# Evictions ahead of the phases, or behind them: one reordered loop in a fused state-space and MLP kernel

## The chip, the cores and the metric

The kernel runs on one core of a Trainium2 chip. The metric is the device time of one execution in microseconds (us), and the median of several executions is what is compared. The core's engines run side by side, each through its own list of instructions in a fixed order, and they meet only at semaphores: TensorE (PE in the profile, its weight loads PEld), VectorE (DVE), ScalarE (ACT), GpSimd (POOL) and SyncE (SP), which here only issues transfers.

## What is computed

The reference is a block with two branches, with one row of conditioning `c` that scales and shifts both (2048 positions, 512 channels, 128 states). Cut to what matters:

```python
mod = silu(c) @ w_mod                       # six rows of 512: sa, ca, ga, sb, cb, gb
h = layernorm(u) * (1 + ca) + sa
K = real(sum_n C * dt*B * exp(dt*A * l))    # a kernel of 2048 taps for each channel
x = u + ga * (causal_conv(h, K) + h * Dskip)
h = layernorm(x) * (1 + cb) + sb
x1 = h + shift(gelu(layernorm(h) @ w1)) @ w2
x = x + gb * (x1 + gelu(layernorm(x1) @ w3) @ w4)
```

`dt` is `exp(log_dt)`; `A`, `B` and `C` are complex. The reference does the convolution with FFTs of length 4096; the kernel does it with matrix multiplications by small DFT matrices.

## The kernel before, in words

All of it is fp32, with products split in two parts where accuracy asks for it. It goes in this order: a preparation (to about 46 us); the **generation stage** (about 46 to 258 us), which makes the 512 x 2048 taps of K and, beside it, normalises u and takes the first DFT of u; the spectra and their products; the inverse transforms; the two halves of the MLP.

The change is in the generation stage. Its loop (L530) runs `k` from 0 to 32; steps 0 to 31 each make the taps of one group of 16 channels of a quarter, and every fourth step is `fresh` (k = 1, 5, 9, ...), which makes the exponentials for the next four steps. The tasks of one step are these:

- `turns(k, cos)` (L452): eight or ten matmuls into a PSUM tile `xx` of 128 x 1024 (the phases, in turns), which ACT turns into `sn` or `cs` with one Sin (L464, recorded at L118, the helper that all ACT work shares). There are two `xx` tiles. The step works two steps ahead: step k issues the phases of step k + 2.
- `exps` (L240): matmuls into the same `xx` tiles, and an Exp by ACT into `p`. The change from Sin to Exp and back costs a table load on ACT.
- `products(k)` (L469): seven DVE operations that multiply `sn`, `cs` and `p` into `e0` and `e1` (two buffers each).
- `burst(k)` (L493): 64 small matmuls of `e1` by `e0` into `kp`. At odd k the tile is full, and an eviction by ACT (`kp` to `KX`) is put off into the list `later`.
- `u_dft` (L431): eight matmuls of the normalised u into two PSUM tiles `pu`, and an eviction put off into `later`: two ACT copies to `vs`, and four transfers of them to DRAM by SP. There are two `pu` tiles, so one `u_dft` fills both. It runs at the end of 16 of the steps.
- `mod_parts` and `mod_sum` (L213, L222): for three of the six rows of the conditioning, matmuls into `pu` and an ACT copy put off into `later` (to `wm` and `modg`).
- `fill` (L488): matmuls whose result is overwritten.

The lists of the engines are written out by hand: the stage stands under `manual_schedule`, so each engine executes its instructions in the order in which the Python code issues them. The matmuls are issued when a task is called; what a task puts into `later` is issued in the next step, as `now`. PE's order in a step is therefore: phases of k + 2, in a fresh step two of the `exps`, `burst(k)`, in a fresh step the rest of the `exps` with `fill`, then `u_dft` or the rows of the conditioning. ACT's order in a step before the change is: `sn` and `cs` of k + 2, the evictions of the step before, and in a fresh step the Exps.

Of the kernel before, what the change touches and what calls it, by code (L numbers as in the profile page):

```python
# [109 lines left out]
def body(ctx, tc, A):  # L110
# [129 lines left out]
    def exps(t, u0, u1):  # L240
        if u0 == 0:
            PE[t] = [], pe.tile([128, 4, 16, NX1], F32, name="p1")
        p0, p1 = PE[t]
        for u in range(u0, u1):
            x = psx.tile([128, 1024], F32, name="xx")
            if u == 4:
                for i, n in ((0, 512), (512, 64 * NX1)):
                    T.matmul(x[:, i:n], TES[:, t], CE[:, 1024 + i:1024 + n], start=True, stop=True)
                act(p1.rearrange("p u d c -> p (u d c)"), x[:, :64 * NX1], AF.Exp)
                continue  # L250
            l = TES[u * 32:u * 32 + 32, t]
            for i in range(2):
                T.matmul(x[:, i * 512:i * 512 + 512], l, CE[u * 32:u * 32 + 32, i * 512:i * 512 + 512],  # L253
                         start=True, stop=True)
            p0.append(pe.tile([128, 2, 512], F32, name="p0", bufs=6))
            act(p0[u].rearrange("p a b -> p (a b)"), x, AF.Exp)

    def weigh(t):
        q1 = PE[t][1][:, :, :, 8:12].rearrange("p a b c -> p (a b) c")
        V.tensor_mul(q1, q1, WN[:, t * 64:(t + 1) * 64, None].to_broadcast([128, 64, 4]))  # L260
# [191 lines left out]
    def turns(k, cos):  # L452
        t, u = divmod(k, 4)
        r0 = slice(u // 2 * 64, u // 2 * 64 + 64)
        r1 = slice(64 - r0.start, 128 - r0.start)
        l0, l1, c = T0S[r0, t], T1S[r1, t * 2 + k % 2], slice(k % 2 * 512, k % 2 * 512 + 512)
        x = psx.tile([128, 1024], F32, name="xx")
        ops = [(l0, C0[r0, c], l1, C1[r1])] + [(ON[r0, i], MG[r0], ON[r1, i], MG[r1]) for i in (2, 0, 1)[1 - cos:]]
        ops.append((l0, C0N[r0, c], l1, C1N[r1]))
        for i, (la, ma, lb, mb) in enumerate(ops):  # L460
            T.matmul(x[:, :512], la, ma, start=(i == 0), stop=(i == len(ops) - 1))  # L461
            T.matmul(x[:, 512:], lb, mb, start=(i == 0), stop=(i == len(ops) - 1))  # L462
        o = wk.tile([128, 2, 512], F32, name="cs" if cos else "sn", bufs=3)
        act(o.rearrange("p a b -> p (a b)"), x, AF.Sin, scale=-TWO_PI, bias=hpi if cos else 0.0)  # L464
        return o
# [3 lines left out]
    def products(k):  # L469
        t, u = divmod(k, 4)  # L470
        sn, cs = trig.pop(k)
        mg, pt = PE[t][0][u], PE[t][1][:, u]
        e0 = wk.tile([128, 2, 2, 512], F32, name="e0")
        e1 = wk.tile([128, 2, 16, 32], F32, name="e1")
        f2 = lambda z: z.rearrange("p a b -> p (a b)")
        m1 = wk1.tile([128, 16, 32], F32, name="m1")
        V.tensor_mul(m1.rearrange("p d (x y) -> p d x y", x=4),
                     pt[:, :, None, :8].to_broadcast([128, 16, 4, 8]),
                     pt[:, :, 8:12, None].to_broadcast([128, 16, 4, 8]))
        for a in range(2):  # L480
            V.scalar_tensor_tensor(e0[:, 1, a], sn[:, 0], 1.0 - 2.0 * a, mg[:, a], op0=OP.mult, op1=OP.mult)  # L481
        V.tensor_mul(f2(e1[:, 1]), sn[:, 1], f2(m1))
        V.tensor_mul(e0[:, 0], cs[:, 0:1].to_broadcast([128, 2, 512]), mg)
        V.tensor_mul(f2(e1[:, 0]), cs[:, 1], f2(m1))
        return e0, e1


    def fill(n):  # L488
        for _ in range(n):
            T.matmul(KP[1].rearrange("p a b -> p (a b)"), TES[:, 0], CE[:, :512], start=True, stop=True,  # L490
                     skip_group_check=True)

    def burst(k, e0, e1):  # L493
        if k % 2 == 0:
            KP[0] = KP.pop(1) if 1 in KP else psk.tile([128, 8, 64], F32, name="kp")
        kp = KP[0]
        for g in range(4):
            for r in range(2):
                for j in range(4):
                    d = j * 4 + g  # L500
                    T.matmul(kp[32 * j:32 * j + 32, (k % 2) * 4 + g], e1[:, r, d],  # L501
                             e0[:, r, :, d * 32:d * 32 + 32],
                             start=(r == 0), stop=(r == 1), skip_group_check=True)
        if k % 2 == 1:
            g0 = (k // 2) * 8
            later.append(lambda: act(Kq[:, g0 // 64, g0 % 64:g0 % 64 + 8], kp))
# [19 lines left out]
    with tc.manual_schedule():  # L526
        for k in range(2):
            trig[k] = turns(k, 0), turns(k, 1)
        weigh(0)
        for k in range(33):  # L530
            now, later = later, []
            if 1 in KP:
                fill(3)
            if k + 2 < 32:
                trig[k + 2] = turns(k + 2, 0), turns(k + 2, 1)
            for f in now:
                f()
            if k < 32:
                fresh = k % 4 == 1 and k < 28
                if fresh:  # L540
                    exps(k // 4 + 1, 0, 2)
                e = products(k)
                burst(k, *e)
                if fresh:
                    KP[1] = psk.tile([128, 8, 64], F32, name="kp")
                    fill(3)
                    for u in range(2, 5):
                        exps(k // 4 + 1, u, u + 1)
                        fill(2)
                if k % 4 == 3 and k < 28:  # L550
                    weigh(k // 4 + 1)
            for f in side[k]:
                f()
        for f in later:
            f()
        V.tensor_add(Kq[:, :, :, 31], DS.rearrange("p (h g) -> p h g", h=2), Kq[:, :, :, 31])
        T2 = [up.tile([128, 16, 128], F32, name="xu") for i in range(2)]
        load_t2 = lambda i: Y.dma_start(T2[i], A["T2"].rearrange("p (a b) -> p a b", a=32)[:, i * 16:i * 16 + 16])
        load_t2(0)
# [482 lines left out]
```

## Time and profile before

| | us |
|---|---|
| median of 3 executions | 814.51 |
| lowest, highest | 814.46, 819.1 |
| span of the profiled execution | 817.4 |
| PE busy | 725.9 (89%) |
| DVE busy | 511.1 (63%) |
| ACT busy | 339.0 (41%) |

The time of the profiled execution itself is not listed apart; its span is the nearest to it, and it lies between the median and the highest. The span counts from the first to the last instruction. Busy times are of instructions as the profiler recorded them; the ends of matmuls are modelled, so that the busy share of PE is not its share of peak. "PEclk" is the share of the full TensorE clock that was granted. A row of the timeline has the start, the duration, the engine, the line, the operation with its tiles (written from read), and in brackets how long the engine was idle before it and what ended that wait.

### The profile page before, as it was taken

The numbers are of one execution on the slowest core, as the hardware profiler recorded it, in microseconds if no ns is written. First come the engines' busy times: TensorE is split into PE (matmuls) and PEld (weight loads), VectorE is DVE, ScalarE is ACT, GpSimd is POOL, SyncE is SP. The second block draws the span as 40 slices with busy tenths as digits, with TensorE's granted clock in tenths as the row PEclk, the third lists the DMA queues.
The fourth block names the chain that finished last, engine by engine and source line by source line (L and its number), as shares of the span: only waits on it lengthen the run. The fifth ranks groups of instructions, "written<-read, shape, count | busy, mean of one in ns | idle before, by whom it ended". The sixth has DMA issues, their size and how long they took to land. (4 is left out here: it accounts for less than half of the span.)

```text
span 817.4 us, 17349 instructions
## 1 busy us (share of the span) xinstructions
PE 725.9 (89%) x7340; PEld 550.9 (67%) x7340; DVE 511.1 (63%) x883; ACT 339.0 (41%) x540; POOL 92.5 (11%) x186
## 2 busy tenths in 40 slices
PE   3798999889888989999459899999999999999994
PEld 1355555545556956565248788888888888888883
DVE  8999888768765355777479988543526271714211
ACT  3677676656755344453134554221322122222220
POOL 1011111011000000010026331010101010101000
PEclk9999999989998599999769899999999999999997
DMA  8421152421415999495803453010101010101011
GB/s 294 147 53 41 26 145 53 116 68 28 117 40 131 246 250 311 146 307 182 287 1 121 160 177 118 26 53 1 52 1 53 1 52 1 26 1 26 1 26 26
DMA packets 51046, 79.88 MB, mean 98 GB/s; under 512 B 5172, under 2 KB 37816, under 8 KB 49432
## 3 DMA queue, kind: packets, MB, share of 16 engines
q1 hardware_dynamic: 44808, 57.92, 25.6%
q0 software_dynamic: 6160, 20.85, 8.1%
q8 instruction: 58, 0.95, 0.5%
q14 instruction: 20, 0.16, 0.1%
HBM read 52.53 MB, written 26.21 MB: 96 GB/s over the span
## 5 line engine op out<-in xcount | busy, mean ns | idle before, releaser
L871 DVE TENSOR_TENSOR gl<-gf,gh 128x512 fp32r<-128x512 f32 (+1 forms) x48 | 30.4, 644 | 150.5 <-ACT gh L118 150.5
L118 ACT ACTIVATE gf<-pm 128x512 f32<-128x512 f32 (+1 forms) x48 | 27.0, 562 | 182.1 <-PE pm L865 178.4
L865 PE MATMUL pm<-nh,w3l 128*128 128x256 f32 (+1 forms) x352 | 98.5, 280 | 0.0
L864 PE MATMUL pm<-nl,w3h 128*128 128x256 f32 (+1 forms) x352 | 98.5, 280 | 0.0
L863 PE MATMUL pm<-nh,w3h 128*128 128x256 f32 (+1 forms) x352 | 98.4, 279 | 0.0
L876 PE MATMUL pa<-w4h,gh 128*128 128x512 f32 (+1 forms) x176 | 73.8, 419 | 3.2 <-ACT gh L118 0.9
L877 PE MATMUL pa<-w4l,gh 128*128 128x512 f32 (+1 forms) x176 | 69.6, 396 | 0.0
L863 PEld LDWEIGHTS pm<-nh,w3h 128*128 128x128 f32 (+1 forms) x352 | 65.4, 186 | 1.8
L865 PEld LDWEIGHTS pm<-nh,w3l 128*128 128x128 f32 (+1 forms) x352 | 65.4, 186 | 1.1
L864 PEld LDWEIGHTS pm<-nl,w3h 128*128 128x128 f32 (+1 forms) x352 | 65.2, 185 | 0.6
L878 PE MATMUL pa<-w4h,gl 128*128 128x512 f32 (+1 forms) x176 | 64.2, 396 | 0.0
L481 DVE SCALAR_TENSOR_TENSOR e<-sn,p 128x512 f32<-128x512 f32 x64 | 41.3, 686 | 33.5 <-ACT sn L118 14.2
L461 PE MATMUL xx<-MG,ON 64*128 64x512 f32 x160 | 51.0, 416 | 0.0
L462 PE MATMUL xx<-MG,ON 64*128 64x512 f32 x160 | 50.9, 415 | 0.0
L118 ACT ACTIVATE sn<-xx 128x1024 f32<-128x1024 f32 x32 | 32.9, 1027 | 40.9 <-issue 34.4
L884 POOL DMA_DIRECT2D out<-KX x32 | 16.1, 508 | 257.6 <-DVE KX L882 257.5
L876 PEld LDWEIGHTS pa<-w4h,gh 128*128 128x128 f32 (+1 forms) x176 | 33.0, 188 | 17.9 <-ACT gh L118 13.2
L770 PE MATMUL pm<-nl,w1h 128*128 128x256 f32 x128 | 39.0, 305 | 6.6 <-DVE nl L741 6.6
L643 DVE TENSOR_TENSOR ma<-pk,us 128x512 f32<-128x512 f32 x32 | 21.9, 685 | 29.3 <-issue 21.3
L118 ACT ACTIVATE p<-xx 128x1024 f32<-128x1024 f32 (+1 forms) x40 | 37.8, 981 | 5.1 <-PE xx L253 3.3
L501 PEld LDWEIGHTS kp<-e,e 128*32 128x32 f32 x2048 | 30.5, 111 | 13.1 <-issue 8.5
L769 PE MATMUL pm<-nh,w1h 128*128 128x256 f32 x128 | 39.3, 307 | 0.0
(222 smaller groups left out, 1910.7 us busy)
## 6 DMA issues: line engine op xcount, KB each, us to landing
VU<-vs SPq DMA_DIRECT2D x64, 128.0 KB, 2.4
ld<-VU SPq DMA_DIRECT2D x32, 256.0 KB, 8.7
ZT<-z POOLq DMA_DIRECT2D x16, 512.0 KB, 4.4
ld<-ZT SPq DMA_DIRECT2D x16, 512.0 KB, 5.4
wst<-in_w SPq DMA_DIRECT2D x18, 256.0 KB, 3.3
xu<-in_u SPq DMA_DIRECT2D x16, 256.0 KB, 6.6
KX<-in_u SPq DMA_DIRECT2D x16, 256.0 KB, 9.7
GD<-go POOLq DMA_DIRECT2D x16, 256.0 KB, 3.3
```

The source lines that it names most:

```text
L118: return S.activation(out, in_, f, bias=bias, scale=scale)
L461: T.matmul(x[:, :512], la, ma, start=(i == 0), stop=(i == len(ops) - 1))
L462: T.matmul(x[:, 512:], lb, mb, start=(i == 0), stop=(i == len(ops) - 1))
L481: V.scalar_tensor_tensor(e0[:, 1, a], sn[:, 0], 1.0 - 2.0 * a, mg[:, a], op0=OP.mult, op1=OP.mult)
L769: T.matmul(p[:, e], W1h[:, k, c], hi[k], start=(k == 0), stop=False)
L770: T.matmul(p[:, e], W1h[:, k, c], lo[k], start=False, stop=False)
L863: T.matmul(p[:m, e], W3h[:, k, c], hi[k], start=(k == 0), stop=False)
L864: T.matmul(p[:m, e], W3h[:, k, c], lo[k], start=False, stop=False)
L865: T.matmul(p[:m, e], W3l[:, k, c], hi[k], start=False, stop=(k == 3))
L876: T.matmul(acc[i], gh[:m, e, s], W4h[:m, f], start=(f == 0), stop=False)
L877: T.matmul(acc[i], gh[:m, e, s], W4l[:m, f], start=False, stop=False)
L878: T.matmul(acc[i], gl[:m, e, s], W4h[:m, f], start=False, stop=(f == 10))
```

## The change

In each step the put-off evictions (`now`) are issued ahead of the phases of k + 2, where they were issued behind them.

```diff
             now, later = later, []
             if 1 in KP:
                 fill(3)
+            for f in now:
+                f()
             if k + 2 < 32:
                 trig[k + 2] = turns(k + 2, 0), turns(k + 2, 1)
-            for f in now:
-                f()
             if k < 32:
                 fresh = k % 4 == 1 and k < 28
```

What `now` issues are ACT copies and SP's transfers, and the phases issue matmuls and ACT's Sins. So the order changes on ACT alone; the lists of PE, DVE, POOL and SP hold the same instructions in the same order as before. ACT's order in a step becomes: evictions of the step before, `sn` and `cs` of k + 2, and in a fresh step the Exps. Where a table load for Sin follows the Exps, the eviction of `kp` (and of `pu`, in some of these steps) comes ahead of that load.

## The prediction

> **What bounds the kernel now.** I first read the busy times by stretches, to see how large the stage of the change is and which engine fills it.
>
> ```profile
> 46.00:258.00 212.00, 188.09 (x2905) 115.50 (x2901) 169.27 (x259) 141.79 (x165) 20.12 (x32) 0.94 0.28 68
> ```
>
> The columns are the stretch, its length, busy PE, PEld, DVE, ACT and POOL, the granted TensorE clock, DMA share and GB/s. The stage takes 212.0 us. PE is busy for 188.1 of them, DVE for 169.3, ACT for 141.8: PE is the fullest, but has 24 us of gaps. What ends them is in the view of waits, PE's in this stage:
>
> ```profile
> PE pu L438 <- ACT vs L118: 9.0, 7, 2.3
> PE pu L217 <- ACT vs L118: 3.9, 3, 2.3
> PE xx L253 <- ACT cs L118: 3.3, 7, 0.5
> PE xx L253 <- ACT p L118: 2.3, 5, 0.7
> PE pu L224 <- ACT wm L118: 1.9, 2, 1.2
> PE pu L438 <- ACT modg L118: 1.5, 2, 1.3
> ```
>
> (Total us, times, longest.) The first two and the last two are one cause: PE wants a `pu` tile that ACT has not evicted yet. They make 9.0 + 3.9 + 1.9 + 1.5 = 16.3 us in 14 waits, two thirds of PE's gaps. The timeline of ACT for steps 7 to 9 shows why the eviction is late.
>
> ```profile
> 93.41 1.11 ACT L118 ACTIVATE cs<-xx,hpi 128x1024 f32<-128x1024 f32 x1 [0.16 <-ACT sn L118]
> 96.60 1.03 ACT L118 ACTIVATE sn<-xx 128x1024 f32<-128x1024 f32 x1 [2.08 <-PE xx L462]
> 97.75 1.11 ACT L118 ACTIVATE cs<-xx,hpi 128x1024 f32<-128x1024 f32 x1
> 98.77 0.59 ACT L118 ACTIVATE KX<-kp 128x512 f32<-128x512 f32 x1
> 99.24 1.09 ACT L118 ACTIVATE vs<-pu 128x512 f32<-128x512 f32 x2
> 102.68 1.03 ACT L118 ACTIVATE sn<-xx 128x1024 f32<-128x1024 f32 x1 [2.35 <-issue]
> 103.82 1.11 ACT L118 ACTIVATE cs<-xx,hpi 128x1024 f32<-128x1024 f32 x1
> 104.84 1.08 ACT L118 ACTIVATE vs<-pu 128x512 f32<-128x512 f32 x2
> 105.93 1.28 ACT L118 ACT_TABLE_LOAD   x1
> ```
>
> PE in the same time:
>
> ```profile
> 93.25 1.10 PE L501 MATMUL kp<-e,e 128*32 128x64 f32 x64
> 94.28 1.09 PE L438 MATMUL pu<-xu,FU 32*64 32x512 f32 x8
> ...
> 96.11 0.39 PE L461 MATMUL xx<-C0N,T0S 64*128 64x512 f32 x1
> ...
> 97.59 1.10 PE L501 MATMUL kp<-e,e 128*32 128x64 f32 x64
> 99.89 1.57 PE L438 MATMUL pu<-xu,FU 32*64 32x512 f32 x8 [1.20 <-ACT vs L118]
> 101.39 0.50 PE L461 MATMUL xx<-C,T0S 64*128 64x512 f32 x1
> ...
> 102.20 0.39 PE L461 MATMUL xx<-C0N,T0S 64*128 64x512 f32 x1
> ```
>
> The burst of step 7 ends at 94.35 and its `pu` tiles are full at 95.37. ACT is idle from 94.52 to 96.60, but stands at `sn`, whose phases end at 96.50. It copies `kp` and `pu` only after `sn` and `cs`, from 98.77 to 100.33. PE, through with the next burst at 98.69, waits 1.20 us for the tiles. Then ACT idles again, 2.35 us, put down to "issue": `sn` at 102.68 follows the last phase matmul of 102.20 + 0.39. So each waits for the other in turn. The 14 waits of `sn` of this kind:
>
> ```profile
> ACT sn L118 <- issue: 34.4, 14, 4.1
> ```
>
> **The change part by part.** Only ACT's order changes: no instruction is added or taken away, and the transfers of `vs` go out in the same order on SP, only earlier. POOL's queue isn't passed.
>
> *The evictions in the new place.* In step 8, `kp` is copied at 94.52 to 95.11, as its burst is done, and the two `vs` copies (1.09) run from about 95.4 to 96.5. `sn` could start at 96.60 as before. The work of 1.56 us fits into the 2.08 us of idle ACT, with 0.1 us to spare. It is the same at the other places, since on PE the phases always stand right behind the `u_dft`: they take 1.2 us (95.30 to 96.50 here), the copies 1.09. Should the hand-over between engines take 0.1 us more than this, 16 pairs cost 16 x 0.1 = 1.6 us; I charge that. Its ends are 0 and 16 x 1.09 = 17.4 (all copies on the path).
>
> *PE's waits for `pu`.* With the tiles free by 96.5, `u_dft` of step 8 starts at 98.6 without a wait. All 16.3 us go. A waiting `u_dft` also runs longer, since its second half waits for the second copy: 1.57 against 1.09 us above. There are six of 1.57, the first and the last being these:
>
> ```profile
> 73.14 1.57 PE L438 MATMUL pu<-xu,FU 32*64 32x512 f32 x8 [1.20 <-ACT vs L118]
> ...
> 253.41 1.57 PE L438 MATMUL pu<-xu,FU 32*64 32x512 f32 x8 [0.71 <-ACT vs L118]
> ```
>
> That is 6 x 0.48 = 2.9 us.
>
> *The Exps.* In step 9 the table load stands behind `vs` (104.84 to 105.92). Now it follows `cs` at once, up to 1.1 us earlier, and the waits of `exps` for `p` (2.3 us in the rows above) go too; the 3.3 for `cs` stay. After the Exps, `kp` is copied while ACT waits for phases, so the Sin load isn't later.
>
> The sum so far is 16.3 + 2.9 + 2.3 = **21.5 us**.
>
> *What is late next.* DVE. Its waits in the stage:
>
> ```profile
> DVE e L481 <- ACT sn L118: 14.2, 6, 3.9
> DVE e L481 <- PE kp L501: 13.6, 7, 3.7
> DVE e L481 <- ACT cs L118: 5.7, 2, 4.2
> DVE p L260 <- ACT p L118: 4.9, 4, 1.9
> ```
>
> They add to 38.4 us, and each is a wait for ACT or PE, which come earlier. A saving of 21 to 30 us leaves DVE 8 to 17 us of slack; above 38 there is nothing. I charge nothing for it and keep half of the 21.5 as the other end, for lack of slack early on: until 79 us DVE has hardly any.
>
> ```profile
> 46.00:79.00 33.00, 30.36 (x481) 19.05 (x481) 32.45 (x52) 24.27 (x27) 5.00 (x8) 1.00 0.18 44
> ```
>
> *The clock.* The granted clock falls to about half in six stretches:
>
> ```profile
> 82.00:87.00 5.00, 5.00 (x15) 3.15 (x13) 4.96 (x10) 3.19 (x4) 1.43 (x2) 0.66 0.25 55
> 110.00:114.00 4.00, 4.00 (x13) 2.51 (x11) 2.00 (x5) 1.93 (x3) 0.00 (x0) 0.57 0.74 194
> 147.00:152.00 5.00, 5.00 (x72) 3.25 (x70) 3.94 (x7) 1.65 (x2) 1.09 (x2) 0.66 0.01 3
> 175.00:182.00 7.00, 6.92 (x42) 3.67 (x46) 4.49 (x7) 1.77 (x4) 1.09 (x2) 0.53 0.36 77
> 208.00:214.00 6.00, 6.00 (x92) 3.88 (x92) 1.84 (x3) 2.15 (x3) 0.00 (x0) 0.72 0.65 146
> 236.00:241.00 5.00, 4.93 (x34) 2.92 (x38) 2.40 (x3) 1.53 (x3) 0.00 (x0) 0.66 0.51 107
> 260.00:287.00 27.00, 27.00 (x492) 25.92 (x486) 10.30 (x16) 8.98 (x18) 0.00 (x0) 0.51 1.05 256
> ```
>
> The lost time is length x (1 - clock). The last four in the stage each follow a long wait for `pu`, as at 175:
>
> ```profile
> 175.08 2.46 PE L438 MATMUL pu<-xu,FU 32*64 32x512 f32 x8 [2.27 <-ACT vs L118]
> ```
>
> They lose 5 x 0.34 + 7 x 0.47 + 6 x 0.28 + 5 x 0.34 = 8.4 us, the first two 3.4. If the waits bring the stretches on, the 8.4 go with them; that they do is read from what follows what, and isn't shown. I take half, 4.2; the ends are 0 and 8.4 + 3.4 = 11.8. The stretch from 260 belongs to the next stage, whose start looks the same after the change; I leave it.
>
> [...]
>
> Sum: 21.5 + 4.2 - 1.6 = **24 us**. The profiled execution's span, 817.4, is 2.9 above the median of 814.51; taking the saving off its own span gives 793.3, off the median 790.5. I forecast the median: **790.5 us**.
>
> **The rivals.**
> - *The half-clock stretches stay.* For it: the two at 82 and 110 follow no wait for `pu`. Against: the other four do. The clock term is 0: 814.5 - 21.5 + 1.6 = 794.6 us. [...]
> - *All of the lost clock comes back.* 814.5 - 21.5 - 11.8 + 1.6 = 782.8 us. It needs PE to have no larger gaps left, and DVE to follow at 8 us of slack.
> - *DVE takes over.* PE's waits for `pu` come back as waits of the burst for `e`. For it: DVE's 32.45 of 33 us early. Against: 38.4 us of waits later. Half of the ledger: 814.5 - 10.8 = 803.7 us.
> - *Slower: the evictions hold up the phases' Sins.* ACT goes through its list in order, so behind an eviction that waits for a `u_dft` stand `sn` and `cs`; for these wait DVE's products and, through the two `xx` tiles, PE's next phases. If the copies end after the phases rather than 0.1 us before, PE's 16.3 us move from `pu` to `xx` and nothing is won, while the 16 copies of `kp` (0.48 us of ACT's time each, by the starts at 98.77 and 99.24) now go ahead of `sn`: 16 x 0.48 = 7.7, giving 822 us. It decides where the copies' end lies past the phases' end by about a copy's length; in the rows it lies before.
> - *It does nothing*, as ACT's place in line doesn't set PE's waits: 814.5. The rows at 98.77 to 99.89 speak against it.
>
> **How the numbers follow.** Forecast (half the clock term) 0.42; stretches stay 0.20; all clock back 0.15; DVE takes over 0.15; slower 0.04; nothing 0.04. The range should reach from the clock case with a little over (half of its uncertainty below: 781) to just short of the DVE case's centre (803): 781 to 803 leaves out half of that case, the last two and the far end of the clock case, some 0.2. A change of 1% (8 us) is about what a measurement of this kernel can tell from none. All of the first four cases are faster by more than that: 0.92; within 1% 0.04; slower 0.04.
>
> **What would show it.** The stage's stretch should be some 188 us long in place of 212. PE's waits for `vs`, `wm` and `modg` should fall from 16.3 us to under 2, and no `u_dft` should take 1.57. ACT's `sn <- issue` should fall from 34.4 us to under 12, as the evictions fill it. DVE's waits should fall from 38.4 to some 15. The first Exp table loads should stand right behind `cs`. Wrong would be waits of PE for `sn` and `cs` in place of those for `pu`, or waits of the burst for DVE that add to over 8 us, or a clock under 0.94 in the stage.

## The result, and the profile after

| | before | after |
|---|---|---|
| median, us | 815.8 (4 executions) | 783.8 (4 executions) |
| lowest to highest | 814.46 to 819.1 | 783.08 to 784.65 |
| span of the profiled execution | 817.4 | 781.3 |
| from the first burst to the next stage's first matmul | 209.7 | 174.6 |

The ratio is 0.960, with a 95% interval of 0.957 to 0.964: the kernel is 4.0% faster, 32 us. The forecast was 790.5 with a range of 781 to 803; the result lies in it, 6.7 us below the forecast and 1 us from the rival in which all of the lost clock comes back (782.8). The profiled execution of after took 783.08 us for its span of 781.3, so some 1.8 us lie around a span. By the same 1.8 us the profiled execution of before, with its span of 817.4, is the one of 819.1, the slowest of its four. So the two profiles lie 36 us apart where the medians lie 32 apart, and what is read from the profiles below is up to some 4 us more than the medians show.

The last row of the table comes from the first burst in the timeline of PE and from the view of the tile `KX` (duration least, median, most; first and last start), of before:

```profile
49.11 1.10 PE L501 MATMUL kp<-e,e 128*32 128x64 f32 x64
...
L585 PE MATMUL pk<-FK,KX x256: 270/416/471, 258.8 to 284.3; 32*128 32x64 f32 x128
```

and of after:

```profile
50.15 1.10 PE L501 MATMUL kp<-e,e 128*32 128x64 f32 x64
...
L585 PE MATMUL pk<-FK,KX x256: 270/416/417, 224.7 to 251.4; 32*128 32x64 f32 x128
```

The generation stage shrank by 209.7 - 174.6 = 35.1 us. The preparation took 1.0 us more in this execution and the rest 2.0 us less; together that is the 36.1 us between the spans.

The busy times of after by stretches (columns as in the prediction), for the stage and for the start of the next one:

```profile
50.00:225.00 175.00, 167.66 (x2896) 105.91 (x2896) 165.46 (x254) 142.26 (x162) 20.79 (x30) 1.00 0.34 82
224.00:256.00 32.00, 31.34 (x540) 29.32 (x544) 10.72 (x17) 10.14 (x22) 0.00 (x0) 0.52 1.05 279
```

PE is now busy for 96% of the stage and DVE for 95%, at a clock of 1.00: none of the six half-clock stretches is left. The start of the next stage is at half clock as before. PE's waits in the stage of after:

```profile
PE xx L253 <- ACT cs L118: 3.5, 7, 0.5
PE kp L501 <- DVE e L484: 1.9, 1, 1.9
PE pk L585 <- DVE KX L556: 1.2, 1, 1.2
PE xx L461 <- ACT sn L118: 0.6, 2, 0.3
```

No wait for `pu` is among them; there were 16.3 us. The same three steps as in the prediction, ACT and then PE, in the timeline of after:

```profile
90.41 1.12 ACT L118 ACTIVATE cs<-xx,hpi 128x1024 f32<-128x1024 f32 x1 [0.21 <-PE xx L462]
91.42 0.59 ACT L118 ACTIVATE KX<-kp 128x512 f32<-128x512 f32 x1
92.41 1.09 ACT L118 ACTIVATE vs<-pu 128x512 f32<-128x512 f32 x2 [0.40 <-PE pu L438]
93.58 1.03 ACT L118 ACTIVATE sn<-xx 128x1024 f32<-128x1024 f32 x1
94.72 1.12 ACT L118 ACTIVATE cs<-xx,hpi 128x1024 f32<-128x1024 f32 x1
96.72 1.09 ACT L118 ACTIVATE vs<-pu 128x512 f32<-128x512 f32 x2 [0.89 <-PE pu L438]
97.89 1.03 ACT L118 ACTIVATE sn<-xx 128x1024 f32<-128x1024 f32 x1
99.03 1.11 ACT L118 ACTIVATE cs<-xx,hpi 128x1024 f32<-128x1024 f32 x1
100.16 1.28 ACT L118 ACT_TABLE_LOAD   x1
```

```profile
91.28 1.09 PE L438 MATMUL pu<-xu,FU 32*64 32x512 f32 x8
92.29 0.50 PE L461 MATMUL xx<-C,T0S 64*128 64x512 f32 x1
93.09 0.39 PE L461 MATMUL xx<-C0N,T0S 64*128 64x512 f32 x1
...
94.56 1.10 PE L501 MATMUL kp<-e,e 128*32 128x64 f32 x64
95.59 1.09 PE L438 MATMUL pu<-xu,FU 32*64 32x512 f32 x8
```

In these steps ACT waits for PE's `u_dft` (0.40, 0.89), copies as soon as it ends, and is through when the phases are: the phases end at 93.09 + 0.39 = 93.48 and `sn` starts at 93.58, 0.10 us later, as it did before the change. PE goes from burst to `u_dft` to phases without a gap, the second `u_dft` takes 1.09 us in place of 1.57, and the table load stands right behind `cs`.

### The profile page after: what moved, and what is told of

It is laid out like the page before. It is cut to its first block, busy times and chain, and to the rows that moved or that the text cites. A ratio compares the mean times of both kernels' runs of the same rounds, so it can differ in the third digit from the quotient of the medians.

```text
span 781.3 us, 17346 instructions
## 1 busy us (share of the span) xinstructions
PE 708.3 (91%) x7340; PEld 541.8 (69%) x7340; DVE 510.0 (65%) x883; ACT 341.5 (44%) x540; POOL 94.2 (12%) x186
## 4 chain that ended last, share of the span: by engine, by line
PE 34%; DVE 8%; ACT 6%; issue 2%; POOL 1%; DMA 0%; DVEq 0%; POOLq 0%; ACTq 0%
PE pa L876 6%; PE pa L878 5%; PE pa L877 5%; PE pm L865 4%; PE pm L863 3%; PE pm L864 3%; ACT gh L118 3%; ACT gf L118 3%; DVE st L716 2%; PE pT L733 2%; PE ph L820 1%; PE ph L821 1%; PE ph L822 1%; DVE h L721 1%; DVE h L720 1%
## 5 line engine op out<-in xcount | busy, mean ns | idle before, releaser
L118 ACT ACTIVATE gf<-pm 128x512 f32<-128x512 f32 (+1 forms) x48 | 27.0, 562 | 182.1 <-PE pm L865 178.4
L461 PE MATMUL xx<-MG,ON 64*128 64x512 f32 x160 | 47.8, 394 | 0.0
L462 PE MATMUL xx<-MG,ON 64*128 64x512 f32 x160 | 47.7, 393 | 0.0
L878 PEld LDWEIGHTS pa<-w4h,gl 128*128 128x128 f32 (+1 forms) x176 | 33.0, 188 | 8.9 <-DVE gl L871 2.4
L118 ACT ACTIVATE z<-pz 128x512 f32<-128x512 f32 x32 | 17.4, 595 | 49.5 <-issue 36.8
```

Source lines behind the costliest of these rows:

```text
L118: return S.activation(out, in_, f, bias=bias, scale=scale)
L878: T.matmul(acc[i], gl[:m, e, s], W4h[:m, f], start=False, stop=(f == 10))
```

## The experiments

Each ran beside the kernel before, whose medians were 816.2 to 816.9 us there. The ratios are to that kernel; where a run is set against the changed kernel, it is against the 783.8 us above (783.08 to 784.65).

**Which eviction matters.** The list `later` is split in two, one for `kp` and one for `pu`.

The cut shows the edit against the changed kernel; the comments and the left-out lines (in which the list is split) are marked by `#` and `...`.

```diff
...
+            now, later, nowk, laterk = later, [], laterk, []
...
             for f in now:        # vs, wm, modg
                 f()
             if k + 2 < 32:
                 trig[k + 2] = turns(k + 2, 0), turns(k + 2, 1)
+            for f in nowk:       # KX
+                f()
```

> The evictions of `pu` (to vs, wm, modg) ahead of the phases as after the change, those of `kp` behind them as before it. Theory (PE's 16 us of waits for `pu`, and the clock that falls behind them, are the whole effect): 784 to 788 us, no PE wait for `pu`, granted clock of the stage near 1.00. Rival (it is the place of `kp`, which after the change is copied ahead of the table load and of the next Sin): at least a quarter of the 32 us is lost, 792 us or more.

Measured: 783.95 us, ratio 0.960 (0.956 to 0.963), the same as the change as a whole. PE has no wait for `pu` (its waits in the stage are those of after, number for number), and the clock stands at 1.00 through the stage. The opposite, with `nowk` ahead and `now` behind:

> The opposite half: `kp` ahead of the phases, `pu` behind. Theory: `pu` is copied up to 0.48 us earlier in some 8 steps, because `kp` no longer stands before it, and that is all: 8 x 0.48 = 4 us, 808 to 813 us, with PE's waits for `pu` at 12 us or more and the half-clock stretches still there. Rival (`kp` matters by itself): under 800 us.

Measured: 806.46 us, ratio 0.987 (0.983 to 0.991). That is 10 us faster than before, more than the theory's 4 and 1.5 us below its range, but short of the rival's. Its waits of PE:

```profile
PE pu L438 <- ACT vs L118: 7.1, 7, 1.8
...
PE pu L217 <- ACT vs L118: 3.2, 3, 1.8
...
PE pu L224 <- ACT wm L118: 1.4, 2, 0.7
PE pu L438 <- ACT modg L118: 0.8, 1, 0.8
```

They add to 12.5 us, 3.8 less than before: the 4 us of the theory. The rest is clock; the stretches at half clock are three here:

```profile
108.00:114.00 6.00, 6.00 (x26) 4.20 (x27) 4.56 (x9) 3.17 (x5) 0.00 (x0) 0.72 0.59 152
200.00:206.00 6.00, 6.00 (x93) 3.90 (x88) 2.28 (x4) 2.41 (x3) 0.00 (x0) 0.72 0.88 224
228.00:232.00 4.00, 4.00 (x22) 2.63 (x18) 2.13 (x3) 1.02 (x1) 0.00 (x0) 0.57 0.63 134
```

They lose 6 x 0.28 + 6 x 0.28 + 4 x 0.43 = 5.1 us, against 11.8 before. So 3.8 us of waits and 6.7 us of clock make the 10 (the stage is 10.2 us shorter, 199.5). Here a small shortening of the waits goes with the loss of more than half of the lost clock. That the place of `kp` does something by itself, beyond that, isn't borne out: with `pu` ahead already, it adds nothing.

**Where the clock goes.** First the kernel before with work for PE in place of its waits, the late evictions left as they are:

```diff
...
+    pads = {4: 10, 8: 10, 11: 6, 12: 10, 14: 11, 15: 5, 18: 20, ...}
+    def pad():                   # called ahead of the step's u_dft or rows
+        for _ in range(pads[k]):
+            T.matmul(<unused half of kp>, TES[:, 0], CE[:, :256], ...)
...
-            if 1 in KP:
+            if 1 in KP and k % 4 == 2:
                 fill(3)
```

Since `pad` makes a `kp` tile in some odd steps, the added condition keeps `fill` to the steps behind the fresh ones. It lets through three more `fill` matmuls in step 30 (87 in the trace in place of 84).

> The kernel before, in which PE multiplies (into a part of `kp` that is overwritten later) in place of each of its 13 longer waits for `pu`, with as many 256-column matmuls as the wait was long (0.11 us each). The late evictions stay, so the order of the work stays that of before. Theory of the clock (PE's idle time is what brings the half-clock stretches): the stage runs at 0.98 or more and most of the 11.8 us come back, 803 to 808 us. [...]

Measured: 810.81 us, median of 10, from 806.85 to 816.12; ratio 0.994 (0.991 to 0.997). That misses the theory's 803 to 808, though it is 5.7 us below the 816.54 of the kernel before beside it. Its stage in three stretches, and the one wait for `pu` that is left in it:

```profile
50.00:214.00 164.00, 157.92 (x2377) 102.58 (x2367) 140.68 (x217) 116.44 (x134) 18.83 (x29) 1.00 0.29 73
214.00:230.00 16.00, 15.81 (x110) 8.49 (x109) 8.32 (x12) 7.95 (x9) 0.00 (x0) 0.57 0.16 34
230.00:255.00 25.00, 23.79 (x503) 16.15 (x499) 16.92 (x24) 14.63 (x21) 0.00 (x0) 1.00 0.23 50
```

```profile
PE pu L438 <- ACT modg L118: 0.2, 1, 0.2
```

Up to 214 us the clock is 1.00, where it was at half five times before, and it is 1.00 again from 230. Between them it falls once, at a group of Exps, for some 14 us, with PE busy for 15.81 of 16. So with work in PE's waits the six old stretches are gone, which fits the theory; the new one (16 x 0.43 = 6.9 us lost, of the 11.8) does not. PE's wait ahead of it is one of 0.5 us for `cs`. There are seven waits for `cs` in the stage, at the Exps, 3.3 us in all; behind the other six the clock stayed at 1.00, though two of these groups had a wait of 0.65 us for `p` besides. So the length of PE's waits alone doesn't tell where the clock falls. The next two runs start from the changed kernel. In the first `fill` issues nothing:

```diff
-        for _ in range(n):
+        for _ in range(0):
             T.matmul(KP[1]..., TES[:, 0], CE[:, :512], ...)
```

> After the change, without the 84 matmuls of `fill` (about 0.22 us apart, so 18 us of PE's 172), whose results are overwritten. Theory of the clock: PE then idles 2 to 3 us around each of the seven groups of Exps, the clock falls to half there for some 3.4 us each, about 12 us lost against at most 18 us of work: 780 to 790 us with a stage clock of 0.94 or less. Rival (idle time doesn't bring the clock down; PE is the bound of the stage now): the stage gets shorter by what DVE allows, 774 to 779 us at a clock of 1.00.

Measured: 788.3 us, ratio 0.965 (0.961 to 0.969), 4.5 us slower than the changed kernel (its fastest execution, 786.76, is above the other's slowest), though PE has 84 matmuls less to do. The stage takes 178.4 us; its row:

```profile
49.00:228.00 179.00, 166.65 (x2812) 103.46 (x2810) 165.60 (x254) 141.93 (x162) 20.77 (x30) 0.86 0.33 80
```

The clock is 0.86: there is a stretch at half clock behind each of the seven groups of Exps, from 3.4 us (at 104) to 10 us (at 148) long. The 3.4 us each of the expectation are the length of the shorter stretches of before: 5 us at 0.66 there are 3.4 us at 0.50. In the second, `fill` works on 32 rows:

```diff
-            T.matmul(KP[1]..., TES[:, 0], CE[:, :512], ...)
+            T.matmul(KP[1]..., TES[:32, 0], CE[:32, :512], ...)
```

> After the change, with the 84 matmuls of `fill` on 32 rows of TensorE in place of 128: as many, 512 columns each as before, so PE is busy for as long. Theory one (the clock follows PE's idle time alone): 783 to 785 us, stage clock 1.00. Theory two (it follows how much of the array works, so that work on 32 rows counts as little as none): the seven half-clock stretches of the kernel without `fill` come back, 786 to 796 us, stage clock 0.95 or less. Told apart because the start of the next stage, all work on 32 rows, runs at half clock for some 30 us with PE busy throughout.

Measured: 792.86 us, ratio 0.971 (0.968 to 0.975), 9 us slower than the changed kernel. Its stage, the longest stretch in it, and PE's waits:

```profile
49.00:233.00 184.00, 175.55 (x2886) 110.79 (x2882) 165.84 (x254) 141.00 (x162) 20.64 (x30) 0.91 0.32 77
104.00:114.00 10.00, 10.00 (x46) 6.39 (x48) 9.08 (x14) 6.23 (x7) 1.09 (x2) 0.50 0.43 111
```

```profile
PE xx L253 <- ACT cs L118: 3.5, 7, 0.5
PE kp L501 <- DVE e L484: 1.8, 1, 1.8
PE xx L248 <- ACT p L118: 1.0, 5, 0.2
PE xx L461 <- ACT sn L118: 0.3, 1, 0.3
```

With the 1.2 us at the stage's end, which this view leaves out, PE's waits are 7.8 us against 7.2 after the change, of 0.5 us or less but for two, and PE is recorded as busy for all of the 10 us from 104 to 114, at half clock. In the program only the rows that `fill` uses differ. So theory one, by idle time alone, doesn't fit. Theory two does in the main: half clock stands behind five of the seven groups of Exps, not all, and the stage is 183.7 us long. It isn't shown either: `fill` on other rows than the Exps also overlaps with them in this trace, and in the padded run the clock stayed at half for 14 us with `fill` on 128 rows.

I then tried to bring up the clock at the start of the next stage, whose matmuls work on 32 rows each, with one dense matmul in each of its eight rounds:

```diff
         kv = KX.rearrange("p (g x) -> p g x", g=64)
+        T.matmul(ps[0]..., ident, KX[:, :512], start=True, stop=True, ...)
```

> After the change, with one matmul of 128 rows and 512 columns more in each of the eight rounds that open the next stage (its result is overwritten), where the clock is 0.50 for 30 us though PE is busy. Theory two of the clock (the array's use counts): the clock comes up in these rounds, each takes 2.6 to 3.2 us in place of 3.4 in spite of the added work, 775 to 783 us. Theory one: the clock stays at half, and the added matmuls cost up to 1.8 us each, 786 to 799 us.

Measured: 801.59 us, 18 us slower than the changed kernel and at the far side of both expectations:

```profile
226.00:270.00 44.00, 44.00 (x531) 32.07 (x532) 9.78 (x16) 8.40 (x16) 0.00 (x0) 0.50 0.62 156
```

The clock stayed at 0.50. One dense matmul in 5 us didn't bring it up, and at half clock each cost 2.2 us (18 / 8). This run doesn't tell the theories apart, since no denser work than this was run here. Nor is this stage a clean case of little of the array at work: its matmuls come in fours, on four different sets of 32 rows, and the four start within 0.04 us of each other, so that together they span all 128 rows. In after:

```profile
225.54 0.43 PE L585 MATMUL pk<-FK,KX 32*128 32x64 f32 x2
225.57 0.42 PE L585 MATMUL pz<-FK,KX 32*128 32x64 f32 x1
225.58 0.42 PE L585 MATMUL py<-FK,KX 32*128 32x64 f32 x1
```

What else sets this stage apart is that PE loads weights nearly all the time (29.32 of 32 us in the row of after above, against 105.91 of 175 in the generation stage). So the number of rows isn't shown to be why this stage runs at half clock, and the expectations, which took it for work on 32 rows, start from too simple a picture.

**The Exps' table load**, the third term of the sum:

```diff
-            for f in now:
-                f()
+            if k % 4 != 1:
+                for f in now:
+                    f()
             if k + 2 < 32:
                 trig[k + 2] = ...
+            if k % 4 == 1:
+                for f in now:
+                    f()
```

> After the change, but in the seven fresh steps the evictions stay behind the phases, ahead of the Exps' table load, as before. It prices the third term of the sum (2.3 us of PE's waits for `p`). Theory: five of the seven steps have an eviction of `pu` there (two copies in three of them, one in two), the table load comes 0.5 to 1.1 us later in these, 2.3 us are lost: 785 to 788 us, without half-clock stretches. Rival (these steps carry more than their share, since they start the longest chain of ACT and PE): 790 us or more.

Measured: 784.25 us, ratio 0.961 (0.958 to 0.964): in the total no loss that shows, just under the theory's 785 to 788. In the stage the term is there:

```profile
PE xx L253 <- ACT cs L118: 3.5, 7, 0.5
PE xx L253 <- ACT p L118: 2.3, 5, 0.7
PE pk L589 <- DVE KX L560: 1.2, 1, 1.2
PE pu L438 <- ACT vs L118: 0.7, 1, 0.7
```

The 2.3 us for `p` are back to the tenth, and the stage takes 177.2 us (49.3 to 226.5) in place of 174.6. Two smaller changes are in these 2.6 us: the 0.7 us for `pu`, and 1.3 us less of waiting for DVE at `kp` (0.6 in place of 1.9). Part of what hides it in the total is the next stage, which ran at full clock for its first 6 us here and was at half clock for some 20 us in place of some 31:

```profile
226.00:232.00 6.00, 4.72 (x138) 4.57 (x142) 1.89 (x4) 1.57 (x4) 0.00 (x0) 1.00 0.93 265
232.00:253.00 21.00, 20.97 (x386) 20.10 (x388) 8.72 (x14) 7.01 (x14) 0.00 (x0) 0.53 1.04 250
```

Its eight rounds took 24.7 us in place of 26.9. The preparation was 0.9 us shorter and the rest 1.6 us longer in this execution, so that a term of 2 to 3 us can't be read from totals here.

**DVE's slack.** DVE is left with little idle time after the change (4.6 + 1.9 us of waits), so it could have become the bound. The normalisation of u is left out:

```diff
-        side[max(at(i) - 2, 0)].append(lambda i=i: u_stats(i))
-        side[at(i)].append(lambda i=i: u_norm(i))
```

> After the change, with the normalisation of u left out (its 16 statistics and 16 modulations, some 38 us of DVE's 169 in the stage); K is computed as before, y from the raw u. Theory (DVE has slack left, PE and the two-way hand-over with ACT are the bound): 781 to 785 us, no change beyond 1%. Rival (DVE has become the bound, at 169.4 us of work in a stage of some 175): at least 8 us faster, 776 us or less.

Measured: 783.9 us, as the changed kernel. DVE's work in the stage fell by 32 us and the stage stayed at 174.5 us:

```profile
49.00:224.00 175.00, 167.66 (x2900) 106.02 (x2901) 133.79 (x191) 142.30 (x162) 0.00 (x0) 1.00 0.32 82
```

The freed time came back whole as DVE's waits for `sn`, `p` and `kp`. PE is the bound.

**A version that beats both.** If PE is the bound and the clock holds, some of `fill` is too much. All three start from the changed kernel. In `e9` the three `fill` matmuls that open the step behind a fresh one are gone, 21 of 84; `e10` has five dense matmuls in PE's last wait of the stage (1.2 us), in case the clock of the next stage falls because of that wait; `e11` has both.

```diff
-            if 1 in KP:
-                fill(3)
...
+        x = psx.tile([128, 1024], F32, name="xx")
+        for i in range(5):
+            T.matmul(x[:, :512], TES[:, 0], CE[:, :512], ...)
         V.tensor_add(Kq[:, :, :, 31], ...)
```

> After the change, without the three `fill` matmuls that open the step behind each fresh step (21 of 84, some 4.6 us of PE), where the waits that they covered may now be gone. If PE's use stays high enough for the clock: 779 to 783 us, stage clock 1.00, bounded by DVE, which has 6.5 us of waits left in the stage. If these fills are among what holds the clock: one or more half-clock stretches at 1.7 us each, 784 to 790 us.

> After the change, with five matmuls of 128 rows and 512 columns in the 1.2 us in which PE waits, at the end of the stage, for the last addition to K. [...]

> Both of the two edits before: the sum of what they give alone, 776 to 784 us; a candidate to beat the changed kernel.

Measured: `e9` 777.0 us, ratio 0.952 (0.950 to 0.955), with the stage at a clock of 1.00 and 5.0 us shorter (50.0 to 219.6), close to the 4.6 us of the matmuls taken out. That is below the expected 779 to 783; where the rest of the 6.8 us between the medians comes from is open. Its interval doesn't touch that of the change (0.957 to 0.964): it is faster than the changed kernel.

```profile
49.00:218.00 169.00, 162.42 (x2852) 102.22 (x2852) 165.57 (x255) 142.41 (x162) 21.94 (x31) 1.00 0.34 83
```

`e10`: 781.89 us, ratio 0.958 (0.955 to 0.960), not to be told from the changed kernel. Its clock fell at some 233 us in place of 225, but so it did in the run with the fresh steps, which had no such matmuls; so it isn't shown that they moved it. `e11`: 776.68 us, ratio 0.951 (0.948 to 0.954), not to be told from `e9`.

## Why the prediction was right, point by point

The saving was put at 24 us, from 814.51; the medians give 32.0, from 815.8. So the forecast was right on the way and on the main cause, and short by a quarter on the size; the higher median of before hides 1.3 us of that in the time.

- *PE's waits for `pu`, 16.3 us*: right. They are gone, and with the `pu` evictions alone moved the whole gain is there; with `kp` alone, 12.5 us of them stay.
- *The longer `u_dft`, 2.9 us*: right; both that stand in the rows of after take 1.09 us, the second of a pair too, and so do the other 14 in its timeline.
- *The Exps, 2.3 us*: right, and measured by itself: 2.3 us of waits, in a stage that was 2.6 us longer.
- *The new place, 1.6 us charged*: not needed. In the rows shown `sn` starts 0.10 us after the phases' end, as before, though in the stage ACT waits 5.9 us in 10 waits for `u_dft` ahead of the copies.
- *The clock, 4.2 us*: the term that was mis-sized, and the step that failed is "I take half". All six stretches went, 11.8 us, also the two at 82 and 110 that I had set apart because no wait for `pu` stood ahead of them. The ledger of 21.5 plus 11.8 makes 33.3 us; the stage gave 35.1 in the profiles. That all of it came back was on the list as a rival; why is open in part. Ahead of the two at 82 and 110 stand waits of 0.5 us for `cs` and 0.66 us for `p`, which could have brought them on; but they stand in the padded run and in the run with the fresh steps too, and there the clock stays at 1.00.
- *DVE*: right that it isn't the bound, shown by the run without the normalisation of u. Its waits fell further than forecast, from 38.4 to 4.6 us rather than 15 (the 1.9 us ahead of the last addition to K stand in both kernels and aren't in the 38.4), because the stage shrank by the clock's share too.
- *The rivals*: "all of the lost clock comes back" held, at 782.8 against 783.8. The slower one would have shown as PE's waits for `sn` at `xx`; these are 0.6 us, as before.

## What to carry to other kernels

Where an engine with a fixed order stands at an instruction whose input comes late, look for work behind it whose input is long there, above all work that frees a buffer for the engine that it waits for: here the same copies, 1.6 us at a time, fitted into idle time that ACT had anyway. When such waits of TensorE go, count the clock as well: here a third of the stage's gain (11.8 of 35 us) was clock. And once they are gone, see which of the matmuls that only keep TensorE busy can go too: without 21 of them the stage was 5 us shorter, without all 84 it was 3.9 us longer.

## What was not expected of the hardware

- The clock fell to half with TensorE recorded as busy: behind `fill` on 32 rows (10 us at 0.50, PE busy for 10.00), and through the first rounds of the next stage (0.50 to 0.53 for 21 to 44 us in these runs). With `fill` on 128 rows it stayed at 1.00 for 175 us in the changed kernel, but fell for 14 us in the padded one. What the clock follows stays open.
- The start of that half-clock time in the next stage moved by some 8 us between runs (225 after the change, 233 in `e5` and `e10`), and the eight rounds there took 24.7 to 30.3 us (`e5`, and the run without `fill`): an effect of 2 to 3 us in the stage is seen in the stage's length and not in the total.
- Work that was taken from TensorE made the kernel slower by 4.5 us (`fill` left out). By an estimate from the stage's row the clock lost 179 x 0.14 = 25 us, where 84 matmuls, some 0.22 us apart, make 18.
